# A two-pass channel scaling kernel: a third less folding scratch, folded rows in the PSUM banks, and joined loads in pass two

## Chip, cores, metric

One core of one Trainium2 chip (trn2). The metric is the device time of one execution in microseconds, median over several. "Fast" is the normal state of a run. The engines are called PE (matmul), DVE (vector), ACT (scalar), POOL and SP; SP issues nearly all transfers here.

## The reference

```python
x: (1, 384, 384, 384) bf16, w1d: (1,) bf16          # H = W = C = 384
g = jnp.einsum("bhwc->bc", x) / (H * W)             # mean of each channel
s = jax.nn.sigmoid(g * w1d[0])                      # one tap
return x * s[:, None, None, :]
```

x is 113.2 MB and every element is needed twice: once for the means, once for the product. What does not fit on chip between the two uses is read from HBM a second time.

## The kernel before

x is taken as 1152 rows of 384 channels in each of the 128 partitions; a row across all partitions is 98,304 bytes. Pass one reads all rows and sums them on PE. Rows that are still on chip at the end of it (kept rows) are only stored in pass two, the others are loaded again, scaled by DVE and stored.

There are three ways to keep a row. A raw row lies in SBUF as it is. Rows in PSUM lie in seven banks that the matmul does not use. And a folded group hides a fourth row in three: x is small, so four exponent bits of each element hold nothing that could not be put back (a test finds elements for which this is false, and a slow path then redoes the rows). DVE spreads the sixteen bits of the fourth row over those places with shifts, masks and XOR, and takes them out again in pass two.

```python
    QS = [16, 16, 16, 8]
    PIECE = 4
    PS = 18
    base, areas = 0, []
    for q in QS:
        areas.append((base, 3 * q))
        base += 3 * q
    RAW = {}
    for name, n in (("A", 59), ("Y", 16), ("U", 16), ("T", 16)):
        RAW[name] = (base, n)
        base += n
    ROWS = base
```

QS are the folded groups (each number counts hidden rows), PS the rows in PSUM, A the raw rows, and Y, U and T the scratch for folding, which is filled with raw rows last.

```python
    def fold(k):
        g, lo, p = pieces[k]
        _, w, wc = area(g, lo, p)
        wall = wc[0] + wc[1] + wc[2]
        ua, ta, ya = U + lo, T, Y
        u, uc = flat(ua, p), rows(ua, p)
        for i, (op, by, mask) in enumerate(
            ((SHL, 4, 0x7800), (SHL, 8, 0x7800), (SHL, 12, 0x7000), (SHR, 4, 0x0800))
        ):
            bits(flat(ta + i * p, p), u, op, by, AND, mask, uc, rows(ta + i * p, p))
        bits(flat(ya, 3 * p), w, AND, 0x7800, XOR, 0x3800, wall, rows(ya, 3 * p))
        bits(flat(ya + 3 * p, p), u, AND, 0x7800, XOR, 0x3800, uc, rows(ya + 3 * p, p))
        join(w, w, flat(ta, 3 * p), XOR, wall + rows(ta, 3 * p), wall)
        w2 = w[:, 2 * p :, :]
        join(w2, w2, flat(ta + 3 * p, p), XOR, wc[2] + rows(ta + 3 * p, p), wc[2])
        y = flat(ya, 4 * p)
        fl.add(
            "ACT",
            lambda: nc.scalar.activation(out=y, in_=y, func=ACTF.Copy, accum_out=seen[:, k : k + 1]),
            reads=rows(ya, 4 * p), writes=rows(ya, 4 * p) + [("seen", k)],
        )
...
    def unfold(k, at):

        g, lo, p = pieces[k]
        a, w, wc = area(g, lo, p)
        w0, w1, w2 = (w[:, j * p : (j + 1) * p, :] for j in range(3))
        ba, ca = Y, Y + PIECE
        u, b, c = flat(at, p), flat(ba, p), flat(ca, p)
        uc, bc, cc = rows(at, p), rows(ba, p), rows(ca, p)
        bits(u, w0, SHR, 4, AND, 0x0780, wc[0], uc)
        bits(b, w1, SHR, 8, AND, 0x0078, wc[1], bc)
        bits(c, w2, SHR, 12, AND, 0x0007, wc[2], cc)
        join(u, u, b, OR, uc + bc, uc)
        bits(b, w2, SHL, 4, AND, 0x8000, wc[2], bc)
        join(u, u, c, OR, uc + cc, uc)
        wall = wc[0] + wc[1] + wc[2]
        bits(w, w, AND, 0x87FF, OR, 0x3800, wall, wall)
        join(u, u, b, OR, uc + bc, uc)
        scale(a, 3 * p)

        bits(u, u, XOR, FIX, AND, 0xFFFF, uc, uc)
        scale(at, p)
```

All engines' orders are fixed when the program is built: a little clock in the kernel plays pass two in advance and decides when DVE scales, when it unfolds, and when each load and store is issued. In the kernel before, this is where free rows are loaded again, one freed region at a time:

```python
        while free and todo < N_STREAM:
            a, n = free.popleft()
            n = min(n, N_STREAM - todo)
            chunk = (todo, n)
            todo += n
            load(chunk, a)
            cuts = list(range(0, n, 16)) + [n]
            parts = [
                (chunk, a, lo, hi, release(a, n) if hi == n else None, 0) for lo, hi in zip(cuts, cuts[1:])
            ]
            moves.append([now + LAT, n * ROW, lambda parts=parts: landed.extend(parts)])
```

One queue (SP) issues loads and stores in the order of that plan, and a load waits there for the store that frees its rows.

## Time and profile before

| what | before |
|---|---|
| time | 734.56 us, median of 3 runs (734.4 to 735.1) |
| span of the profiled run | 731.8 us |
| bytes moved | 305.4 MB, mean 418 GB/s |
| DVE busy | 429.7 us (59%) |
| row transfers | 89 loads, 64 stores |

The rows that carry the reading (busy shares, slices, windows, the chain at the turn, the DVE forms) are shown in the prediction. In the rows of slices each digit is the busy share of one fortieth of the span, in tenths. "DMA share" is the mean busy share of the 16 transfer engines, 1.00 when all of them are full; "the turn" is the place between the two passes, where the sum must be complete before anything can be stored.

### The profile page before, as it was taken

The numbers are of one execution on the slowest core, as the hardware profiler recorded it, in microseconds if no ns is written. First come the engines' busy times: TensorE is split into PE (matmuls) and PEld (weight loads), VectorE is DVE, ScalarE is ACT, GpSimd is POOL, SyncE is SP. The second block draws the span as 40 slices with busy tenths as digits, with TensorE's granted clock in tenths as the row PEclk, the third lists the DMA queues.
The fourth block names the chain that finished last, engine by engine and source line by source line (L and its number), as shares of the span: only waits on it lengthen the run. The fifth ranks groups of instructions, "written<-read, shape, count | busy, mean of one in ns | idle before, by whom it ended". The sixth has DMA issues, their size and how long they took to land.

```text
span 731.8 us, 3048 instructions
## 1 busy us (share of the span) xinstructions
PE 215.6 (29%) x1200; PEld 120.6 (16%) x1200; DVE 429.7 (59%) x355; ACT 81.3 (11%) x37; POOL 0.2 (0%) x4
## 2 busy tenths in 40 slices
PE   3976868779899760000000000000000000000000
PEld 1543434445455330000000000000000000000000
DVE  0000001959599219699899968999798724229320
ACT  2000000747477200000000000000000000000000
POOL 0000000000000000000000000000000000000000
PEclk9898998999899995555555555555555555555555
DMA  9999999999999969999999999999999999999996
GB/s 387 420 431 433 434 426 435 422 431 424 427 418 424 422 264 374 412 430 425 429 421 434 440 412 433 431 436 430 416 442 428 412 441 430 426 427 437 436 422 281
DMA packets 22047, 305.62 MB, mean 418 GB/s; under 512 B 2450, under 2 KB 2450, under 8 KB 5522
## 3 DMA queue, kind: packets, MB, share of 16 engines
q1 hardware_dynamic: 22032, 305.44, 98.5%
q8 instruction: 9, 0.15, 0.1%
q14 instruction: 4, 0.03, 0.0%
q10 hardware_dynamic: 2, 0.00, 0.0%
HBM read 192.18 MB, written 113.25 MB: 417 GB/s over the span
## 4 chain that ended last, share of the span: by engine, by line
DMA 46%; DVE 27%; another core or an unknown queue 9%; PE 9%; ACT 5%; issue 0%; SPq 0%
DMA arena<-in_x_dram 28%; DVE arena L414 18%; DMA out_dram<-arena 18%; PE bank L227 8%; DVE arena L262 6%; ACT arena L302 4%; DVE arena L268 2%; PE bank L242 0%; DVE arena L470 0%; SPq L221 0%; ACT s_bf L405 0%; SPq L424 0%; SPq L677 0%; SPq L112 0%
## 5 line engine op out<-in xcount | busy, mean ns | idle before, releaser
L414 DVE TENSOR_TENSOR arena<-arena,s_bf 128x6144 bf16<-128x6144 bf16 (+6 forms) x96 | 236.7, 2515 | 117.5 <-DMA arena<-in_x_dram 86.8
L227 PE MATMUL bank<-arena,ones 128*128 128x384 bf16 x1152 | 207.9, 344 | 54.3 <-DMA arena<-in_x_dram 54.3
L262 DVE TENSOR_SCALAR arena<-arena 128x1536 uint16<-128x1536 uint16 x168 | 108.1, 687 | 148.4 <-DMA arena<-in_x_dram 137.8
L227 PEld LDWEIGHTS bank<-arena,ones 128*128 128x128 bf16 x1152 | 115.9, 102 | 145.9 <-DMA arena<-in_x_dram 58.8
L302 ACT ACTIVATE arena<-arena 128x6144 uint16<-128x6144 uint16 x14 | 74.5, 5324 | 157.3 <-DVE arena L262 157.3
L268 DVE TENSOR_TENSOR arena<-arena 128x1536 uint16<-128x1536 uint16 (+1 forms) x70 | 89.1, 1273 | 0.5
L490 PE MATMUL bank<-odd,ones 128*128 128x1 bf16 x1 | 0.2, 188 | 57.8 <-DVE odd L485 57.8
L490 PEld LDWEIGHTS bank<-odd,ones 128*128 128x128 bf16 x1 | 0.1, 106 | 58.2 <-DVE odd L485 58.2
L242 PE MATMUL bank<-ones,zeros 128*128 128x384 bf16 x46 | 7.8, 326 | 0.0
L470 DVE TENSOR_TENSOR arena<-bank,s_bf 128x768 bf16<-128x768 bf16 (+2 forms) x15 | 5.1, 392 | 1.7 <-DMA out_dram<-arena 1.6
L242 PEld LDWEIGHTS bank<-ones,zeros 128*128 128x128 bf16 x46 | 4.5, 98 | 3.0
L334 ACT COPY bank<-arena 128x512 uint32<-128x512 uint32 (+1 forms) x7 | 3.6, 567 | 5.6 <-DMA arena<-in_x_dram 5.6
L405 ACT ACTIVATE s_bf<-bank,w_sc 128x384 bf16<-128x384 f32 x1 | 0.6, 581 | 27.6 <-PE bank L227 27.6
L302 ACT ACTIVATION_READ_ACCUMULATOR arena<-arena 128x1 f32 x14 | 2.6, 186 | 0.0
L650 ACT ACT_TABLE_LOAD x1 | 1.3, 1283 | 0.7 <-PEq L666 0.7
L313 PE MATMUL bank<-w_bf,ones 1*128 1x1 bf16 x1 | 0.2, 181 | 2.1 <-DMA w_bf<-in_w1d_dram 2.1
L318 DVE TENSOR_SCALAR w_sc<-bank 128x1 f32<-128x1 f32 x1 | 0.2, 160 | 1.1 <-PE bank L313 1.1
L308 DVE MEMSET ones<- 128x128 bf16 x1 | 0.2, 165 | 1.0 <-SPq L106 1.0
L313 PEld LDWEIGHTS bank<-w_bf,ones 1*128 1x128 bf16 x1 | 0.1, 99 | 2.1 <-DMA w_bf<-in_w1d_dram 2.1
L494 DVE CAST odd_i<-bank 128x1 int32<-128x1 f32 x1 | 0.2, 157 | 0.3 <-PE bank L490 0.3
L485 DVE TENSOR_SCALAR odd<-worst 128x1 bf16<-128x1 f32 x1 | 0.2, 156 | 0.0
L480 DVE TENSOR_REDUCE worst<-seen 128x1 f32<-128x14 f32 x1 | 0.2, 159 | 0.0
(5 smaller groups left out, 0.5 us busy)
## 6 DMA issues: line engine op xcount, KB each, us to landing
arena<-in_x_dram SPq DMA_DIRECT2D x17, 4608.0 KB, 39.1
arena<-in_x_dram SPq DMA_DIRECT2D x23, 1536.0 KB, 20.0
out_dram<-arena SPq DMA_DIRECT2D x7, 4608.0 KB, 41.8
out_dram<-arena SPq DMA_DIRECT2D x20, 1536.0 KB, 22.3
out_dram<-arena SPq DMA_DIRECT2D x12, 2304.0 KB, 35.8
arena<-in_x_dram SPq DMA_DIRECT2D x11, 2304.0 KB, 26.3
arena<-in_x_dram SPq DMA_DIRECT2D x20, 1152.0 KB, 15.6
arena<-in_x_dram SPq DMA_DIRECT2D x10, 1056.0 KB, 19.1
```

The source lines that it names most:

```text
L227: return nc.tensor.matmul(acc, lhsT=ones[:], rhs=arena[:, i, :], start=first, stop=last)
L242: lambda: nc.tensor.matmul(acc, lhsT=zeros[:], rhs=ones[:, None, :].to_broadcast([P, C // P, P]), start=False, stop=False),
L262: lambda: nc.vector.tensor_scalar(out=dst, in0=src, scalar1=s0, scalar2=s1, op0=op0, op1=op1),
L268: "DVE", lambda: nc.vector.tensor_tensor(out=dst, in0=a, in1=b, op=op), reads=reads, writes=writes
L302: lambda: nc.scalar.activation(out=y, in_=y, func=ACTF.Copy, accum_out=seen[:, k : k + 1]),
L313: lambda: nc.tensor.matmul(votes, lhsT=ones[0:1, :], rhs=w_bf[0:1, 0:1], start=True, stop=True),
L334: lambda bk=bk, lo=lo, hi=hi: nc.scalar.copy(bk[:, 0 : hi - lo].bitcast(u32), psflat[:, lo:hi].bitcast(u32)),
L405: lambda: nc.scalar.activation(out=s_bf[:], in_=acc, func=ACTF.Sigmoid, scale=w_sc[:, 0:1]),
L414: lambda: nc.vector.tensor_tensor(out=v, in0=v, in1=s_bf[:, None, :].to_broadcast([P, n, C]), op=Op.mult),
L470: lambda sv=sv, dv=dv, by=by: nc.vector.tensor_tensor(out=dv, in0=sv, in1=by, op=Op.mult),
L490: lambda: nc.tensor.matmul(votes, lhsT=ones[:], rhs=odd[:], start=True, stop=True),
L650: nc.scalar.preload_act_table(ACTF.Sigmoid)
```

## The change

The intent is to keep more rows on chip, so that fewer are read twice, and to move the rest in fewer transfers. Y, U and T shrink from 16 rows to 8 each and a second U of 8, called V, joins them, so the scratch goes from 48 rows to 32; folding one piece is done in two rounds through it. These 16 rows and 20 of the raw rows A become one more folded group and a part of another: 36 more stored rows, which hide 12. The 18 rows in PSUM become a folded group too, with 6 hidden rows. In pass two, adjacent free rows are joined, and a load waits until 32 are free or little is queued.

```diff
-    QS = [16, 16, 16, 8]
+    QS = [4, 16, 16, 16, 16]
     PIECE = 4
-    PS = 18
+    Q_BANKS = 6
 ...
-    for name, n in (("A", 59), ("Y", 16), ("U", 16), ("T", 16)):
+    for name, n in (("U", 8), ("V", 8), ("A", 39), ("Y", 8), ("T", 8)):
 ...
+    BANKED = len(QS)
+    PS = 3 * Q_BANKS
+    QS.append(Q_BANKS)
+    areas.append((A, PS))
 ... (fold: two rounds, two tests of 8 rows each)
+        test(0, [(a, 2 * p)])
+        field(0, SHL, 4, 0x7800)
+        field(1, SHL, 8, 0x7800)
+        w01 = flat(a, 2 * p)
+        join(w01, w01, t, XOR, wc[0] + wc[1] + tc2, wc[0] + wc[1])
+        test(1, [(a + 2 * p, p), (ua, p)])
+        field(0, SHL, 12, 0x7000)
+        field(1, SHR, 4, 0x0800)
+        w2 = flat(a + 2 * p, p)
+        for i in range(2):
+            join(w2, w2, flat(T + i * p, p), XOR, wc[2] + rows(T + i * p, p), wc[2])
 ... (pass two: the rows in PSUM are copied back by ACT, then unfolded; unfolding can be
 ...  interrupted by scaling)
-        while free and todo < N_STREAM:
-            a, n = free.popleft()
-            n = min(n, N_STREAM - todo)
 ...
+        if got and todo < N_STREAM:
+            n, a = max(got)
+            n = min(n, CAP, N_STREAM - todo)
+            ahead = backlog()
+            if n >= BIG or n == N_STREAM - todo or (ahead < LOW and n >= 8) or ahead < LAST:
```

Here `got` lists the runs of adjacent free rows, and BIG, CAP, LOW, LAST are 32 rows, 48 rows, 9 us and 4 us. Cuts are marked by "...".

## The prediction

> **What bounds the kernel now.** I began with the page's busy shares, then its forty slices, to see whether one engine limits throughout or several in turn.
>
> ```profile
> PE 215.6 (29%) x1200; PEld 120.6 (16%) x1200; DVE 429.7 (59%) x355; ACT 81.3 (11%) x37; POOL 0.2 (0%) x4
> ...
> DVE  0000001959599219699899968999798724229320
> ...
> DMA  9999999999999969999999999999999999999996
> GB/s 387 420 431 433 434 426 435 422 431 424 427 418 424 422 264 374 412 430 425 429 421 434 440 412 433 431 436 430 416 442 428 412 441 430 426 427 437 436 422 281
> ```
>
> No engine reaches two thirds of the span, while the DMA row is 9 everywhere but in two slices: one near 265 us, where the sum over all of x must end before anything may be stored, and the last one. DVE stands at 8 or 9 from slice 18 to 31, so the second pass has little to spare there. Next, the windows view with the program cut at those two places (window, length, then busy us of PE, PEld, DVE, ACT, POOL, clock, DMA share, GB/s):
>
> ```profile
> 20.00:264.00 244.00, 200.89 (x1136) 113.41 (x1135) 99.85 (x112) 75.83 (x28) 0.00 (x0) 0.94 1.00 427
> 264.00:290.00 26.00, 6.91 (x42) 3.74 (x40) 17.53 (x12) 0.58 (x1) 0.00 (x0) 0.74 0.74 276
> 290.00:720.00 430.00, 0.19 (x1) 0.11 (x1) 311.96 (x229) 0.00 (x0) 0.00 (x0) 0.50 1.01 429
> 720.00:732.00 12.00, 0.00 (x0) 0.00 (x0) 0.00 (x0) 0.00 (x0) 0.00 (x0) 0.50 0.43 183
> ```
>
> In both passes the transfer engines are full at 427 to 429 GB/s. At the turn they lose 0.26 x 26 = 6.8 us, at the end 0.57 x 12 = 6.8 us. The kernel is a stream of bytes with two holes in it, so a change can act on three things only: bytes, cost per transfer, holes. The chain of waits, followed from its last piece back through the turn, says what the turn hole is made of:
>
> ```profile
> 247.03 19.37 DMA arena<-in_x_dram
> 266.40 0.05 issue
> 266.45 5.39 PE bank L227 x32
> 271.83 0.02 issue
> 271.86 0.59 ACT s_bf L405
> 272.45 0.02 issue
> 272.47 22.39 DVE arena L414 x13
> ```
>
> The last long load lands, 32 rows are summed after it, the sigmoid takes 0.59 us, and DVE must scale five rows before the first store can go.
>
> **What the Trainium skill says.** "DMA: Bandwidth & Descriptors", section "Where 436 GB/s comes from", puts the ceiling of the 16 engines at 435 GB/s, yet says that transfers with HBM are held at about 358. The trace contradicts the latter and sits 2% under the former. "HBM Reference", section "Specifications (TRN2)", gives about 425 for a core that streams alone, which agrees with the 427 to 429. Back on the first page, "Why small descriptors are slow (HBM only)" charges each packet a fixed overhead; the packet records below show one. "VectorE: DVE Perf Modes", section "The perf-mode tier table", lets a two-tensor operation on 16-bit data run at half the rate of one with a scalar. The view of groups by form agrees: from 1536 to 4608 elements the first grows by 1599 ns, the second by 802.
>
> ```profile
> L262 DVE TENSOR_SCALAR arena<-arena 128x1536 uint16<-128x1536 uint16 x140 | 71.6, 554 | 146.8 <-DMA arena<-in_x_dram 137.8 <-DMA out_dram<-arena 8.4
> L268 DVE TENSOR_TENSOR arena<-arena 128x1536 uint16<-128x1536 uint16 x56 | 53.3, 953 | 0.5
> L262 DVE TENSOR_SCALAR arena<-arena 128x4608 uint16<-128x4608 uint16 x28 | 38.0, 1356 | 1.6
> L268 DVE TENSOR_TENSOR arena<-arena 128x4608 uint16<-128x4608 uint16 x14 | 35.7, 2552 | 0.0
> ```
>
> **The change part by part.** x has 1152 rows per partition, of 768 bytes each. All are read once and all written once; those that could not stay on chip are read again. Folding hides every fourth row in spare exponent bits of three others, so four rows take the room of three.
>
> *Bytes.* Kept before: 18 rows in PSUM + 4 x 56 folded + 107 raw = 349, so 803 are read again. Kept after: 4 x 74 (the group in PSUM included) + 71 raw = 367, so 785. The on-chip store is 275 rows both times; the gain is 3 x 4 + 6 = 18 rows, because 12 more stored rows hold folded data and the 18 PSUM rows carry 6 hidden ones. Total row movements fall from 1152 + 803 + 1152 = 3107 to 3089.
>
> *Cost of a row and of a transfer.* In the trace's record of every packet, the mean is 1367 ns at 36,864 bytes, 688 at 18,432, 468 at 12,288, 352 at 9216 and 241 at 6144. The slope is (1367 - 468) / 24,576 = 0.0366 ns per byte, and some 15 ns stay over at each size. Each transfer is 128 packets, eight per engine, plus a 9 ns one, so a row costs 8 x 768 x 0.0366 = 0.225 us and a transfer 8 x 15 + 9 = 0.13 us. Eighteen rows: 4.05 us. The instruction lists have 153 row transfers before and 138 after (89 to 82 loads, 64 to 56 stores): 15 x 0.13 = 1.95 us. **Together 6.0 us**, all of it on the path, since DMA is the path. As a check, the same two costs give 3107 x 0.225 + 153 x 0.13 = 719 us for the kernel before, against 720.5 us of recorded packet time per engine and a span of 731.8.
>
> *Folding, pass one.* Before, a four-row piece has five short scalar operations, one long, one long and one short join: 5 x 0.55 + 1.36 + 2.55 + 0.95 = 7.6 us of DVE, 14 pieces, 107 us. After, with half the scratch, the work goes in two rounds: one 8-row test (about 0.96, between the two forms above), six short scalar operations, one 8-row join (1.75, the mean of the scaling form with 3072 elements) and two short ones: 0.96 + 3.3 + 1.75 + 1.9 = 7.9 us. For 74 / 4 = 18.5 piece equivalents that is 146 us, or 39 more. ACT's test is halved in size and doubled in number, each about 2.9 us (half of 5.32, plus 0.19 to read the accumulator). It fits beside 3.8 us of other DVE work, so a pair of pieces needs about 16 us. Pairs arrive every 71 to 97 rows, at 0.227 us a row with its share of transfer costs: 16.1 us at the closest. So it stays **hidden, with no margin to speak of**.
>
> *Unfolding, pass two.* The chain shows 9.8 us per piece, its own scaling included. 18.5 pieces take 181 us; 785 reread rows at 0.20 us and some 55 instruction starts of 0.15 make 165; the 71 raw rows 16. In all 362 us of DVE in a pass of about 440, against roughly 330 before. The seven PSUM copies go to idle ACT (0.58 us each).
>
> *The turn.* The last rows now come in blocks of 8, 8, 8, 5 and 3 rather than 16, 16, 8, 5, 3, and the first store needs four scaled rows, not five. I allow **0.8 us**: about 5 rows less of PE backlog at 0.168, no more. The end hole I leave alone: it is 16 engines finishing unevenly.
>
> *Sum.* 734.56 - 6.0 - 0.8 = 727.8; I round down to 727.5.
>
> **The rivals.**
> 1. *DVE binds.* For it: 8s and 9s in the second pass and 70 us more DVE work. Against it: 362 of 440, with DVE idle for more than half of 600 to 700 us before. If unfolding delays scaling until the store queue runs dry, a few us return: 730 to 735.
> 2. *The issue queue stalls.* One in-order queue issues loads and stores; joined loads wait for 32 free rows or a nearly empty backlog, so a late store now delays a big load. For it: the queue already waited 165.8 us for stores to finish. Against it: transfers stayed at share 1.01 all the same. Cost if true: 2 to 6 us, 730 to 734.
> 3. *The fold delays the turn.* The last scratch rows are reloaded only after the last fold; 86 rows (19.5 us) separate them, against 16 us of fold plus about 3 us of latencies. A slip here opens the hole by 1 to 4 us.
> 4. *The holes shrink too.* Finer pieces could refill the queue sooner after the turn. The windows around 282 to 290 us show full share at a poor rate; if that goes too, 723 to 725.
>
> **Range and chances.** Byte and transfer savings are near certain (6 us). Rivals 1 to 3 can only give back, at most about all of it; rival 4 can add 3 or 4. That gives 722 to 733.5. Faster by 2% would mean under 719.9, which is 7.9 us beyond the sum: 0.04. Slower by 2% means over 749.3, that is, a schedule broken for 20 us: 0.02. Within 2%: 0.94.
>
> **What would show it.** Bytes moved must be 303.7 MB and packets about 1900 fewer for 15 transfers. DMA share should stay at 1.00 in both passes and the slope of packets unchanged. DVE busy should rise to about 505 us, ACT in all to some 115 us. The DMA idle at the turn should be 5.5 to 7 us. I am wrong if share falls below 0.98 over 50 us of pass two (rivals 1, 2), if loads before the turn wait for DVE or ACT for longer than they take to be hidden (rival 3), or if the span falls by more than packet time does (rival 4).

## The result, and the profile after

728.22 us, median of 4 runs (728.05 to 729.99), against 734.55 of the kernel before. The ratio is 0.9918, 95% interval 0.9901 to 0.9935. (A ratio here is the mean time of one kernel's fast runs over the mean of the other's in the same rounds, so it is not quite the ratio of the medians quoted.) A second set gave 729.08 against 734.86, ratio 0.9926, interval 0.9912 to 0.9939. So some 6 us were gained, under 1%.

| what | before | after |
|---|---|---|
| row transfers | 153 | 138 |
| bytes moved | 305.4 MB | 303.7 MB |
| packet time per engine, whole run | 721.4 us | 716.2 us (second set), 717.3 (first) |
| of it in pass two | 453.9 us | 448.2 us, 449.0 |
| DVE busy | 429.7 us | 496.2 us |
| ACT busy | 81.3 us | 115.4 us |
| sigmoid starts at | 271.86 us | 271.93 us, 271.97 |

Packet time is the sum of the recorded durations of all DMA packets, over 16; pass two starts with the issue of the first store. The page of the first profiled run, after (busy shares, then rows of the forty slices):

```profile
PE 211.9 (29%) x1202; PEld 118.1 (16%) x1202; DVE 496.2 (68%) x469; ACT 115.4 (16%) x92; POOL 0.2 (0%) x4
...
DVE  4600007887985729998999997999969993355330
...
DMA  9999999999999978999999999999999999999996
GB/s 379 426 433 436 425 419 429 430 430 427 426 422 424 409 315 334 415 420 428 431 415 442 421 428 426 427 442 430 417 425 438 434 434 427 421 433 448 419 430 273
```

DVE now stands at 9 for most of pass two and works already in the first two slices of pass one (the group for PSUM), yet the DMA row is as before: full, with the same two holes. The windows view of the second set's run, cut as in the prediction (length, busy us of PE, PEld, DVE, ACT, POOL, clock, DMA share, GB/s), says the same in numbers. Its last window is longer than what is left of the span.

```profile
20.00:264.00 244.00, 194.12 (x1110) 108.47 (x1109) 128.98 (x177) 102.47 (x79) 0.00 (x0) 0.96 1.00 426
264.00:290.00 26.00, 7.50 (x44) 3.92 (x42) 17.14 (x15) 0.58 (x1) 0.00 (x0) 0.75 0.76 292
290.00:720.00 430.00, 0.00 (x0) 0.00 (x0) 340.44 (x262) 3.99 (x7) 0.00 (x0) 0.50 1.00 428
```

Both passes run at share 1.00, at the rate of before. The turn is idle for 0.24 x 26 = 6.2 us (5.7 in the first set), against 6.8. The chain of waits at the turn, in the first profiled run (start, length, what):

```profile
256.51 2.87 ACT arena L290 x2
259.38 0.02 issue
259.39 9.72 DMA arena<-in_x_dram
269.11 0.05 issue
269.16 2.79 PE bank L226 x16
271.95 0.02 issue
271.97 0.59 ACT s_bf L423
272.56 0.02 issue
272.58 14.84 DVE arena L432 x8
```

It runs through the last test of the last fold on ACT, as rival 3 of the prediction feared, into the load of that scratch. But the load then took 9.72 us to land: loads issued before it landed one after another up to 267.2 us, and the DMA share from 255 to 264 us was still 0.99 (first profiled run). The fold was on the chain without opening a hole.

```profile
255.00:264.00 9.00, 6.09 (x36) 3.10 (x35) 4.11 (x7) 3.27 (x4) 0.00 (x0) 1.00 0.99 406
```

PE sums 16 rows after the last wait, not 32, and still the sigmoid begins no earlier. Last, the new forms in the view of groups, to compare with the durations that the prediction put in:

```profile
L290 ACT ACTIVATE arena<-arena 128x3072 uint16<-128x3072 uint16 x36 | 99.5, 2763 | 146.5 <-DVE arena L250 146.5
L256 DVE TENSOR_TENSOR arena<-arena 128x3072 uint16<-128x3072 uint16 x18 | 31.6, 1758 | 7.7 <-PE bank L226 6.4
L250 DVE TENSOR_SCALAR arena<-arena 128x3072 uint16<-128x3072 uint16 x18 | 17.3, 960 | 90.8 <-DMA arena<-in_x_dram 89.0 <-ACT arena L290 0.6
```

The join was put at 1750 ns and the test's DVE part at 960.

From profile to profile the span fell by 4.8 us (to 727.0, second set) and 3.6 us (to 728.2, first), packet time by 5.2 and 4.1. So the span did not fall by more than packet time, which was to be the sign of rival 4. The profiled run of the kernel before was one of its fastest (733.62 us), so these differences lie below those of the medians.

### The profile page after: what moved, and what is told of

It reads as the page before. It is cut to its first block, busy times and chain, and to the rows that moved or that the text cites. A ratio compares the mean times of both kernels' runs of the same rounds, so it can differ in the third digit from the quotient of the medians.

```text
span 728.2 us, 3243 instructions
## 1 busy us (share of the span) xinstructions
PE 211.9 (29%) x1202; PEld 118.1 (16%) x1202; DVE 496.2 (68%) x469; ACT 115.4 (16%) x92; POOL 0.2 (0%) x4
## 4 chain that ended last, share of the span: by engine, by line
DMA 56%; DVE 27%; PE 6%; another core or an unknown queue 4%; ACT 2%; SPq 1%; issue 0%; DVEq 0%
DMA arena<-in_x_dram 41%; DVE arena L432 18%; DMA out_dram<-arena 16%; PE bank L226 6%; DVE arena L250 5%; DVE arena L256 4%; ACT arena L290 2%; SPq L220 1%; ACT s_bf L423 0%; PE bank L504 0%; DVE odd L499 0%; DVE odd_i L508 0%; DVE worst L494 0%; DVEq L112 0%
## 5 line engine op out<-in xcount | busy, mean ns | idle before, releaser
L432 DVE TENSOR_TENSOR arena<-arena,s_bf 128x1536 bf16<-128x1536 bf16 (+8 forms) x102 | 241.8, 2411 | 74.9 <-DMA arena<-in_x_dram 60.8
L250 DVE TENSOR_SCALAR arena<-arena 128x1536 uint16<-128x1536 uint16 (+2 forms) x247 | 145.8, 633 | 116.5 <-DMA arena<-in_x_dram 104.1
L226 PE MATMUL bank<-arena,ones 128*128 128x384 bf16 x1152 | 203.7, 338 | 57.8 <-DMA arena<-in_x_dram 57.8
L226 PEld LDWEIGHTS bank<-arena,ones 128*128 128x128 bf16 x1152 | 113.2, 101 | 148.0 <-DMA arena<-in_x_dram 63.8
L256 DVE TENSOR_TENSOR arena<-arena 128x1536 uint16<-128x1536 uint16 (+2 forms) x114 | 121.0, 1061 | 8.5 <-PE bank L226 6.4
L290 ACT ACTIVATE arena<-arena 128x3072 uint16<-128x3072 uint16 (+1 forms) x38 | 102.5, 2696 | 147.8 <-DVE arena L250 147.8
L360 ACT COPY arena<-bank 128x512 uint32<-128x512 uint32 (+1 forms) x7 | 4.0, 570 | 70.7 <-DMA out_dram<-arena 70.6
L290 ACT ACTIVATION_READ_ACCUMULATOR arena<-arena 128x1 f32 x38 | 7.1, 186 | 0.0
```

Source lines behind the costliest of these rows:

```text
L226: return nc.tensor.matmul(acc, lhsT=ones[:], rhs=arena[:, i, :], start=first, stop=last)
L250: lambda: nc.vector.tensor_scalar(out=dst, in0=src, scalar1=s0, scalar2=s1, op0=op0, op1=op1),
L256: "DVE", lambda: nc.vector.tensor_tensor(out=dst, in0=a, in1=b, op=op), reads=reads, writes=writes
L360: "ACT", lambda: nc.scalar.copy(dst.bitcast(u32), src.bitcast(u32)), reads=reads, writes=writes
L432: lambda: nc.vector.tensor_tensor(out=v, in0=v, in1=s_bf[:, None, :].to_broadcast([P, n, C]), op=Op.mult),
```

## The experiments

The theory: the gain is bytes and transfers, and the added engine work is hidden. The rivals: the unfolding on DVE takes part of the gain back; folding takes part of it at the turn; joined loads stall the queue; the turn has more to give. Twelve runs were made, each against the kernel before on its chip. "The changed kernel" below is the second set, 729.08 us. Differences in microseconds are of medians on that same chip; the runs "lessdve", "fold2" and "turn" ran on another chip and are compared by their ratios to the kernel before.

### The yardstick

Edit: none. The changed kernel again.

> The changed kernel once more, as the yardstick for the runs beside it. Byte theory (18 rows at 0.225 us and 15 transfers at 0.13 us): 728.2 us, ratio to the kernel before 0.992, DMA packet time per engine near 717 us. If the first profile of it (729.99 us) is what is typical instead, 730 us and 0.994.

Measured: 729.08 us (727.96 to 729.98), ratio 0.9926. Its runs spread over 2 us, so the 729.99 of the first profiled run is inside the normal spread and needs no cause. It also sets what can be resolved: differences under about 1 us cannot.

### Bytes: no group in PSUM, and half a group

```diff
-    Q_BANKS = 6
+    Q_BANKS = 0      # "bank0", with guards for an empty group
+    Q_BANKS = 3      # "bank3"
```

> No group in the PSUM banks at all: 24 more rows are read again (809), 137 transfers, and DVE has 6/74 less folding and unfolding to do. Byte theory: 24 x 0.225 - 0.13 = 5.3 us more than the changed kernel, about 733.5 us. DVE theory (the second pass is held by unfolding): DVE is relieved by some 24 us, so the time rises by less than 3 us or falls.

> Half the group in PSUM (9 stored rows with 3 hidden): 12 more rows read again (797), 146 transfers. Byte theory: 12 x 0.225 + 8 x 0.13 = 3.7 us more than the changed kernel, about 731.9 us; by bytes alone without the cost per transfer 2.7 us, about 730.9. DVE theory: under 1.5 us more, or less time.

Measured: 733.87 us with none (ratio 0.9987, interval 0.9973 to 1.0000), 4.8 us more than the changed kernel; 731.78 us with half (0.9961), 2.7 us more. Per row read again that is 4.8 / 24 = 0.20 us, and 2.7 / 12 = 0.23 us before anything is taken off for the eight more transfers of the half group (0.17 to 0.19 after it, at the costs found below). In the first of the two, packet time in pass two rose from 448.2 to 453.6 us, 5.4 us, which is 24 x 0.225; in the second to 452.5, 4.3 us and more than the clock shows. The rows cost what was predicted, within the resolution, and less folding work brought no relief that shows. With the whole PSUM group gone, nearly all of the change's gain is gone too. Not quite all: this kernel reads six rows more than the kernel before (809 against 803) in 16 transfers fewer, which by the costs found here is a loss of 1.35 us less 0.7 to 1.2; its median was 1.0 us lower (interval 0 to 2.0). About 1 us of the gain may thus come from something else that this kernel shares with the changed one, such as the new order of pass two. No run takes that apart.

### The cost of a transfer: the same bytes in pieces

```diff
+    SPLIT = 8
 ...
-            known.append(store(chunk, a, lo, lo + n))
+            for e, f in split(n, SPLIT):
+                known.append(store(chunk, a + e, lo + e, lo + f))
 ...
-                load(chunk, a)
+                for e, f in split(n, SPLIT):
+                    load(chunk, a + e, e, f)
```

> Same bytes, same order, but every load and store of pass two is issued in pieces of at most 8 rows: 318 transfers in place of 138. Cost per transfer of 0.13 us on the path: 180 x 0.13 = 23.4 us more, about 751.6 us, all of it in packet time. If the fixed part of a packet lies beside other packets: no change, 728 to 730 us. If the issuing queue cannot follow: well over 23 us more, with DMA share under 0.97 in pass two.

Measured: 737.29 us, ratio 1.0038 (1.0023 to 1.0054): 8.2 us more, between the two expectations of none and 23.4. A transfer cost 8.2 / 180 = 0.046 us, a third of what the prediction took. The recorded packet time rose from 716.2 to 729.3 us, by 13.0: more than the clock did. The windows line for pass two of this run shows how that can be:

```profile
290.00:720.00 430.00, 0.00 (x0) 0.00 (x0) 341.77 (x263) 4.00 (x7) 0.00 (x0) 0.50 1.02 421
```

The share stands at 1.02: the records of neighbouring packets overlap, so part of a packet's recorded fixed time lies beside the next packet. It is an upper bound of what a transfer costs. The rate fell from 428 to 421 GB/s.

### Joined loads undone

```diff
-    BIG, CAP, PART, LOW, LAST = 32, 48, 16, 9.0, 4.0
+    BIG, CAP, PART, LOW, LAST = 8, 16, 16, 9.0, 4.0
```

> Pass two joins no free rows: loads of at most 16 rows, as soon as 8 are free. Same bytes, 119 loads and 91 stores, 210 transfers in place of 138. Byte theory with the cost per transfer that the split run gave (8.2 us / 180 = 0.046 us): 72 x 0.046 = 3.3 us more than the changed kernel, about 732 us; with the predicted 0.13 us: 9.4 us, about 738. Rival, that long loads make the issuing queue stall: the short ones come out even or faster.

Measured: 734.73 us, ratio 0.9999 (0.9984 to 1.0014): 5.7 us more for 72 transfers, 0.078 us each, between the two costs expected. Packet time rose by 6.1 us (722.3 from 716.2), so much of this is service of smaller packets. But recorded packet time overstates here too, and in this run's profile the hole at the end is larger: over the last 25 us of the span the DMA share is 0.65, against 0.74 in the changed kernel, some 2.2 us more idle time. Without it 3.5 us are left, 0.048 each, as in the split run; whether that hole is there in every execution is not shown, so 0.078 is the upper end. Short loads were not faster, so the rival that long ones stall the queue finds no support. It does not say that joining by itself gained 5.7 us over the kernel before, which had 153 transfers and not 210.

### More and less work for DVE in pass two

```diff
-            bits(c, w2, SHR, 12, AND, 0x0007, wc[2], cc)
+            for _ in range(1 + 4):          # "unfold4"; 1 + 8 in "unfold8"
+                bits(c, w2, SHR, 12, AND, 0x0007, wc[2], cc)
```

The repeats write the same values again; the order of everything else is unchanged. The plan does not know of the added work. In "lessdve", that line and the `join(u, u, c, ...)` that uses it are left out, so the three lowest bits of the fourth row's elements come out wrong; the transfers are the same.

> Four idle repeats of one short DVE operation in each unfolded piece: 4 x 0.55 x 18.5 = 41 us more DVE work in pass two, order unchanged. Byte theory: hidden, within 1.5 us of the changed kernel. DVE theory (rival 1): a good part of the 41 us shows, 10 us or more.

> Eight repeats: 83 us more DVE work in pass two, some 425 of 450 us busy. If the slack can be used wherever it lies: under 3 us more. If the early part of pass two has little slack, as its 9s in the page suggest: 10 to 40 us more. DVE theory: about 80 us more.

> Wrong result on purpose: two operations (0.55 + 0.95 us) are left out of each unfolded piece, 28 us less DVE work in pass two; transfers and order unchanged. If DVE costs the changed kernel nothing (DMA share 1.00 to 1.01 all through pass two): within 1 us of it, about 728.5 us. If DVE already holds it, as the last 15 us of the run with four repeats might mean: 3 us faster or more, under 726.

Measured: 743.35 us with four repeats (1.0118), 14.3 us more than the changed kernel; 784.95 with eight (1.0684), 55.9 us more; 728.96 with work left out, ratio 0.9926, the same ratio as the changed kernel's own. So less work gained nothing (28 us by the plan; DVE busy in pass two fell by 21 us in the trace), 41 us more cost 14, and the next 41 us cost 42. The first added dose alone would have spoken for rival 1, as expected beforehand, and the second, at 55.9, fell between two expectations (10 to 40, and about 80); it took the run with less work to show that DVE does not bind the kernel as it is. That is a kink: free up to 41 - 14 = 27 us, and 82 - 56 = 26 us by the second run, then one for one, if the cost has one kink, which two doses cannot test. **DVE does not hold the changed kernel, but with this order of pass two it is some 26 us from doing so.** The windows view shows where, first in the changed kernel, then with four repeats (DVE is the third busy column, DMA share and GB/s the last two):

```profile
290.00:590.00 300.00, 0.00 (x0) 0.00 (x0) 284.34 (x241) 3.99 (x7) 0.00 (x0) 0.50 1.01 428
590.00:720.00 130.00, 0.00 (x0) 0.00 (x0) 56.10 (x22) 0.00 (x0) 0.00 (x0) 0.50 1.00 430
```

```profile
420.00:425.00 5.00, 0.00 (x0) 0.00 (x0) 5.00 (x3) 0.00 (x0) 0.00 (x0) 0.50 0.36 149
...
595.00:600.00 5.00, 0.00 (x0) 0.00 (x0) 5.00 (x3) 0.00 (x0) 0.00 (x0) 0.50 0.44 186
600.00:605.00 5.00, 0.00 (x0) 0.00 (x0) 5.00 (x2) 0.00 (x0) 0.00 (x0) 0.50 0.27 116
```

The last unfolding operation starts at 594.1 us, so nearly all of it lies before 590, and there DVE is idle for only 300 - 284.3 = 15.7 us. The other 74 idle us come after, where next to nothing is left to unfold. (The kink lies 10 us beyond those 15.7; what covers the rest, rows already scaled and waiting in the queue perhaps, was not tested.) With 41 us more, DVE is full at 420 and 600 us while the DMA share falls to 0.27: the queue has run out of scaled rows.

### The same load on the kernel before

```diff
-        bits(c, w2, SHR, 12, AND, 0x0007, wc[2], cc)
+        for _ in range(1 + 5):
+            bits(c, w2, SHR, 12, AND, 0x0007, wc[2], cc)
```

> The kernel before with five idle repeats in each unfolded piece: 5 x 0.55 x 14 = 39 us more DVE work in pass two, near the 41 us that cost the changed kernel 14 us. From 290 to 590 us DVE was idle for 33 us in the kernel before and for 16 us in the changed one. If that idle time is the usable slack: some 5 to 8 us more than the kernel before. If the change did not spend slack: 14 us more, as in the changed kernel.

Measured: 737.99 us against 734.52, ratio 1.0040: 3.5 us for 39 us of added work, where the changed kernel paid 14.3 for 41, and less than the 5 to 8 expected from the idle time. If the same kink holds, which this one dose does not test, the kernel before had some 35 us to spare. The change did spend slack, about 9 us of it, though DVE's work in pass two (290 to 720 us) grew by 28 us, from 312 to 340. Why so little of the 28 is missing from the slack is not settled; the order of pass two was rewritten as well.

### More work for DVE in pass one

```diff
-        field(1, SHL, 8, 0x7800)
+        for _ in range(1 + 4):          # "fold4"; 1 + 2 in "fold2"
+            field(1, SHL, 8, 0x7800)
```

> Four idle repeats of a short DVE operation in each folded piece of pass one: a pair of pieces takes 20.4 us in place of 16, while pairs come every 16 to 22 us. No margin, as predicted: the backlog grows to some 13 us and the last scratch rows are reloaded 18 us later, so the turn is 13 to 18 us later. With the 6 us that the trace shows between the last fold and the first packet of the load that waited for it: about 11 us later. If folding has plenty of room: under 1.5 us.

> Two idle repeats in each folded piece (1.1 us a piece, 18.2 us a pair) in place of four. No margin, as predicted: 2 to 4 us later. With some 6 us between the last fold and the packets that waited for it: hidden, within 1 us of the changed kernel.

Measured: with four repeats 737.68 us (1.0042), 8.6 us more (about 11, or 13 to 18, was expected if there was no room); with two, 729.83, ratio 0.9928 (0.9911 to 0.9945), the same as the changed kernel. Four repeats open the hole that rival 3 described. The window 264 to 270 us, in the changed kernel and then with four repeats:

```profile
264.00:270.00 6.00, 5.42 (x33) 2.90 (x32) 0.00 (x0) 0.00 (x0) 0.00 (x0) 1.00 0.75 303
```

```profile
264.00:270.00 6.00, 2.96 (x19) 1.56 (x16) 5.79 (x10) 2.74 (x3) 0.00 (x0) 1.00 0.01 4
```

DVE and ACT are still folding, nothing is transferred, and the sigmoid starts at 280.18 us, not 271.93: 8.25 us, nearly the whole loss. Two repeats, 2.2 us a pair, cost nothing. So folding has a margin of between 2.2 and 4.4 us per pair of pieces. The traces show it directly: in the changed kernel DVE waits 7.0 and 3.9 us for rows to land in the last two pairs (at 224.6 and 244.1 us), with two repeats 2.9 and 1.7 us, with four not at all.

### Finer first stores at the turn

```diff
-    landed.append((c_raw, Y, Y - U, 4, False))
-    landed.append((c_raw, Y + 4, Y - U + 4, 4, True))
-    landed.append((c_raw, T, T - U, 8, True))
-    landed.append((c_raw, U, 0, 8, True))
+    for a in (Y, Y + 2):
+        landed.append((c_raw, a, a - U, 2, False))
+    for a in (Y + 4, T, T + 4, U, U + 4):
+        landed.append((c_raw, a, a - U, 4, a in (Y + 4, T + 4, U + 4)))
```

> The first stores after the turn go in pieces of 2, 2, 4, 4, 4, 4, 4 rows in place of 4, 4, 8, 8. First store packet some 0.4 us earlier, the thin share of the next 4 us filled, 3 transfers more: about 0.5 to 1 us faster than the changed kernel, some 728 us. If the turn is bound by something else: no change.

Measured: 728.95 us (727.78 to 730.19), ratio 0.9921 (0.9907 to 0.9935) against 0.9926 for the changed kernel. The first store was issued 1.20 us after the sigmoid began, in place of 1.60, as expected; whether any of those 0.4 us reached the end is below what the runs resolve. It was the one try at a version that beats both kernels, and it is not shown to.

## Why the prediction was right

727.5 us was predicted, 728.22 and 729.08 were measured, and the range held both. By its own steps:

- **The bound.** Right. (One reading on the way is loose: from slice 18 to 31 the DVE row has a 6 and a 7 among its 8s and 9s.) DMA share stayed at 1.00 in both passes, and taking DVE work away changed nothing.
- **Bytes, 4.05 us.** Right within the resolution: 0.17 to 0.20 us per row on the clock, transfers taken off, against 0.225, and 5.4 us of packet time for 24 rows. The prediction's reason for the 18 rows has a slip: 36 more stored rows hold folded data, not 12; they hide 12 more rows, so the 18 stand. The traffic is the predicted 303.7 MB.
- **Transfers, 1.95 us.** Too large. The mechanism is there, but 0.13 us each was read from packet records that overlap. The runs gave 0.046 and at most 0.078, so 15 transfers are worth 0.7 to 1.2 us. (The packet count fell by 2157, not about 1900: each transfer has 16 small packets besides its 128.)
- **The turn, 0.8 us.** Did not come on the clock, though 6.2 and 5.7 us of idle transfer time are within the 5.5 to 7 foretold. The sigmoid starts at 271.93 to 271.97 us against 271.86. Pass one also has three more transfers, and its packet time is 0.5 to 0.9 us longer.
- **The sum.** With bytes as predicted and transfers as measured it is 4.05 + 0.7 to 1.2 = 4.8 to 5.3 us, against 5.8 by the medians of the second set; the interval of its ratio is 4.5 to 6.5 us. The prediction's own sum was 6.8 us (then rounded to a forecast of 7), too large by up to 2 us in the two small terms. The total came out 0.5 to 1 us from the measured one because the big term is right and, by luck, because the gain lies somewhat above what the measured terms give. (With the row costs measured on the clock, 3.1 to 3.6 us in place of 4.05, they give still less.) Whether that last 0.5 to 1 us or more is more than spread is open; the run without a PSUM group leaves a similar remainder.
- **Folding hidden, "with no margin to speak of".** Hidden is right; no margin is wrong. Two more operations a piece cost nothing. The arithmetic set 16 us a pair against the closest spacing of 16.1, but the last pairs come 19.5 us apart (224.6 and 244.1 us), and DVE waits for them. It also left out that the last load waits behind others that are already queued.
- **Rival 1, DVE.** It does not bind. The sum was close (362 us; the trace has 357.6 after 272 us), and DVE busy in all rose to 496.2 us where 505 was foretold. But the argument from it (362 of 440 us) overstated the room: that is 78 us, and 26 can be used, since the idle time after 590 us comes too late for unfolding.
- **Rival 2, the queue.** No sign of it: the share stayed at 1.00 and undoing the joins made pass two slower.
- **Rival 4, the thin rate after the turn.** It is there in both kernels, at another place, and was not removed.

## What to carry to other kernels

When transfers fill the span, count rows first: bytes predicted this change better than anything else. Take a cost per transfer from a run that splits the same bytes, not from packet records, which can overlap. And before a next step of the same kind, ask how much idle time of an engine lies where the work could still use it: here 74 of 90 idle microseconds of pass two lay past the point where unfolding ends. Then add work until it costs, since idle time alone said 16 us where 26 could be spent.

## What the Trainium skill lacked or had wrong

- "DMA: Bandwidth & Descriptors", section "Where 436 GB/s comes from", says that the HBM side, at about 358 GB/s, binds transfers between HBM and SBUF, though the same passage points to a measurement of 425. For one core alone the sentence does not hold: it ran at 426 to 430 GB/s for hundreds of microseconds, reading and writing, near the 425 for a single core that the prediction cites.
- The same page, section "Why small descriptors are slow (HBM only)", gives a fixed overhead per packet, but does not say that packet records overlap. 180 more transfers added 13.0 us of recorded packet time per engine and 8.2 us of time, at a share of 1.02.
- No page has what happens where the first loads join the stores after the turn: the transfer engines are as busy as ever at 0.5 to 0.7 of the rate. The windows view of the kernel before, then of the changed one (first set), shows it; the cause was not tested.

```profile
284.00:288.00 4.00, 0.00 (x0) 0.00 (x0) 4.00 (x3) 0.00 (x0) 0.00 (x0) 0.50 0.97 300
```

```profile
288.00:290.00 2.00, 0.00 (x0) 0.00 (x0) 2.00 (x5) 0.00 (x0) 0.00 (x0) 0.50 1.03 204
```
